# A fused attention, gated layer and soft mixture: a new order of the first loads and reductions, and a later place for the turn of P

## The chip, the cores and the metric

The kernel runs on one core of a Trainium2 chip. The metric is the device time of one execution in microseconds (us); the time of a kernel is the median of its runs. The core has a matrix engine (TensorE, PE in the profile, with its weight loads as PEld), VectorE (DVE), ScalarE (ACT), GpSimd (POOL) and a queue that issues most of the DMAs (SyncE, SP).

## The reference

Three layers follow each other. q, k and v have 8 batches, 12 heads, 448 tokens and 64 features per head, all float32.

```
q_n, k_n = rmsnorm(q, g_q), rmsnorm(k, g_k)
attn = softmax(q_n @ k_n.T / 8);  x = attn @ v             # per batch and head
x = (sigmoid(x @ w_gate) * (x @ w_val)) @ w_out            # 768 -> 1536 -> 768
logits = x @ phi                                           # 3584 x 32
slot_input = softmax(logits over tokens).T @ x
slot_out[e] = relu(slot_input[e] @ w1[e]) @ w2[e]          # 8 experts, 4 slots each
out = softmax(logits over slots) @ slot_out
```

w_gate, w_val and w_out come as float64: the kernel reads their bits as pairs of 32-bit words.

## The kernel before, in words

**Pairs.** Attention is worked in 48 pairs of heads (j, from 0), six to a batch. The first 12 pairs, two batches, are worked in float32: `prep_a` squares q and k (ScalarE for pair 0, GpSimd after that), `prep_b` sums the squares on VectorE (line 272, then a scale on line 275), `prep_c` raises the sums to the power -1/2 on GpSimd (line 305) and scales k, `prep_g` turns q and k with TensorE into tiles named qt, which ScalarE copies to qkt (lines 396 and 400). A pair then has seven score tiles, t0 to t6. Each runs through `score` (TensorE, lines 428 and 434, into a PSUM tile sc; four such buffers are shared with the other tiles of that pool), `soft_max` (VectorE, line 470, which also scales by a factor in ss), `soft_exp` (ScalarE, line 490, into a tile p or ps: two buffers of the first and three of the second, taken in turn), `soft_hi` (the turn of P: four transposes on TensorE, line 499, into a tile pq) and `soft_lo` (a copy out by ScalarE, line 532). When all seven are in, `weigh` sums the rows (rs, lines 576 and 582) and multiplies by v (av, line 590). The other 36 pairs use float16 halves and turn P by DMA.

**Weights.** The three weight matrices are brought from float64 bits to float32 by three VectorE instructions per block (lines 694, 697 and 700), their largest value is found by ScalarE (line 677) and spread over the partitions by a small TensorE product (`spread_max`, line 129, tile am) that VectorE reduces (line 133); then they are split into float16 halves (ScalarE lines 742 and 743, GpSimd line 744). w_gate and w_val come in twelve blocks f of 256 columns, from pair 1 on.

**The largest value of v.** For each batch the kernel needs the largest value of v. For batch 0 `v_first` loads v[0] whole (1344 KB), reduces it on VectorE (line 233), and spreads it with the same `spread_max` on TensorE.

**The gated layer** follows one batch behind: chains of 18 float16 products (line 805), in the order gate f=0, gate f=1, value f=0, value f=1, gate f=2 and so on, each evacuated by ScalarE (line 811, gate) or VectorE (line 816, value). The soft mixture works in between and at the end.

**What sets the order.** The program is an agenda: `at(g, fn)` puts a piece of work on a step g; a pair has 18 steps, or 28 and 16 in the second batch, and a step of the gated layer has six products. The gated layer begins at step M0 = 115. Up to step 259 a scheduler re-orders what the agenda issues, by a simulated time line, on each engine; from there the order is as issued. Each engine's queue is worked in order. Ahead of step 0 stands the beginning, in the order of the words in `ORD`: `sel` builds the identity matrix and the 16 blocks of a selection matrix that only the soft mixture uses, `g` loads the two gain vectors g_q and g_k (tile gl) and makes their product ggn and the scales from it, `qk0`, `qk1`, `v0`, `v1` load pairs 0 and 1, `a0` to `g0` prepare pair 0, `w` starts the first weight loads (tiles wr), `vf` is `v_first`, `phi` loads phi and makes four copies of it.

Of the kernel before, what the change touches and what calls it, by code (L numbers as in the profile page):

```python
# [2 lines left out]
KN=json.loads('{"NPRE": 6, "PS": 15, "GO": -4, "GS": 3, "WOF": 2, "WS": 4, "EW": 4, "RSL": 4, "XF": 12, "NX": 4, "VSPL": 5, "VO": 8, "SQA": 1, "MUV": 1, "LOV": 1, "XS": 144, "SF": 7, "AM": 100, "AMO": 100, "AMG": 100, "LEN": [28, 16, 16, 16, 16, 16], "PO": [0, 0, 5, 9, 10, 11, 15, 3], "SO": [0, 3, 6, 8, 11, 13, 15], "PJ": 8, "LOJ": 6, "LOI": [1, 4], "WN": 68, "GB": 2, "WB": 0, "QW": 0, "QO": 0, "QS": 0, "QL": 0, "PX": 2, "QX": 0, "SX": 1, "TX": 3, "LAG": 99, "TEND": 20, "XSL": [5, 4, 3, 2], "DUP": 2, "ACC": 1, "NWT": 0, "NWP": 1, "JQ": 12, "EQ": [0, 0], "NQV": 1, "ORD": "sel qk0 a0 g qk1 w b0 c0 d0 e0 f0 g0 a1 v0 vf v1 phi", "JP": 12, "EVP": [], "DGE": 0}')  # L3

# [6 lines left out]
F32 = mybir.dt.float32  # L11
# [3 lines left out]
AF = mybir.ActivationFunctionType  # L15
ALU = mybir.AluOpType
# [7 lines left out]
def kernel(  # L24
# [83 lines left out]
    def at(g, fn):  # L108
        agenda.setdefault(max(g, now[0]), []).append(fn)
# [107 lines left out]
    def vamax_spread(b):  # L217
        vam_t["ps", b] = spread_max(vam_t[b][:, 6:7], 1)
# [8 lines left out]
        sig_t[b] = sg  # L227

    def v_first():
        x = gt.rearrange("p f a s -> p (f a s)").bitcast(F32)[:, 0:6 * S]  # L230
        sp.dma_start(out=x, in_=v[0].rearrange("h s d -> (h s d)").rearrange("(p e) -> p e", p=128))
        t = smp.tile([128, 8], F32, tag="vam", name="vam")
        vec.tensor_reduce(out=t[:, 6:7], in_=x, axis=AX.X, op=ALU.max, apply_absolute_value=True)
        vec.tensor_scalar(out=t[:, 6:7], in0=t[:, 6:7], scalar1=1e-30, scalar2=None, op0=ALU.max)
        vam_t[0] = t
        vamax_spread(0)
        vamax_scale(0)

    def moe_scales(b):
        sg = sig_t[b]  # L240
# [1032 lines left out]
    if True:  # L1273
        vec.memset(nhalf1, -0.5)
        EW = KN.get("EW", 1)

        def gains():
            gl = p1.tile([128, 2, D], F32, tag="t3", name="gl", bufs=3)
            for i, g in enumerate((g_q, g_k)):
                sp.dma_start(out=gl[:, i, :], in_=g.unsqueeze(0).to_broadcast([128, D]))  # L1280
            gm = smp.tile([128, 4], F32, tag="wa", name="gm")
            vec.tensor_tensor(out=ggn, in0=gl[:, 0, :], in1=gl[:, 1, :], op=ALU.mult)
            vec.tensor_reduce(out=gm[:, 0:1], in_=ggn, axis=AX.X, op=ALU.max, apply_absolute_value=True)
            vec.tensor_scalar(out=gm[:, 0:1], in0=gm[:, 0:1], scalar1=1e-30, scalar2=None, op0=ALU.max)
            exponent(gm[:, 1:2], gm[:, 0:1])
            vec.reciprocal(out=gm[:, 2:3], in_=gm[:, 1:2])
            vec.tensor_scalar(out=ggn, in0=ggn, scalar1=gm[:, 2:3], scalar2=None, op0=ALU.mult)
            if JQ:
                for i in range(2):
                    vec.tensor_copy(out=gl[:, i, :], in_=ggn)  # L1290
                ps = ps_mm.tile([128, 128], F32, tag="mm", name="gt")
                pe.transpose(out=ps, in_=gl.rearrange("p i d -> p (i d)"), identity=ident)
                act.copy(gcol, ps[:, 0:1])
            for o, sign in ((nesc, -1), (esc, 1)):
# [148 lines left out]
```

## Time and profile before

| | |
|---|---|
| time, median of 3 runs | 1691.48 us (1683.35 to 1693.24) |
| the profiled execution's own time | 1691.47 us |
| its span, from the first to the last instruction | 1689.7 us |
| busy: PE, DVE, ACT, POOL | 1562.3, 1055.4, 936.6, 634.7 us |
| clock of TensorE granted, mean | 0.963 |
| first product of scores | 30.12 us after the span's start |
| first product of the gated layer | 168.2 us |

Outside the span lie 1.77 us of the profiled execution's time, and that time is the median. In a row of a timeline stand the start, the duration in us, the engine, the line of the kernel, the operation, what it writes and reads, and how many instructions were merged (a float32 product counts as two instructions); in brackets, how long the engine sat idle before it and what ended that wait. In a row by windows stand the stretch and its length, then the busy time and the number of instructions of PE, PEld, DVE, ACT and POOL, the granted TensorE clock, the busy share of the DMA engines and what they moved in GB/s.

### The profile page before, as it was taken

How to read it: one execution, taken by the hardware profiler on the slowest of the kernel's cores; microseconds unless marked ns; L12 is line 12 of the kernel's file. 1: busy time of each engine (PE TensorE's matmuls, PEld its weight loads, DVE VectorE, ACT ScalarE, POOL GpSimd, SP SyncE). 2: the span in 40 equal slices, each digit the busy share in tenths (PEclk: the TensorE clock that was granted, in tenths of full speed). 3: DMA queues.
4: the chain of work that ended last, by engine and by line, in shares of the span. 5: the costliest groups of instructions: out<-in, count | busy, mean ns of one | idle time of the engine just before them, and what ended most of it. 6: DMA issues, size and time to landing. Idle time of an engine off the chain costs nothing.

```text
span 1689.7 us, 26467 instructions
## 1 busy us (share of the span) xinstructions
PE 1562.3 (92%) x9065; PEld 777.8 (46%) x9065; DVE 1055.4 (62%) x2602; ACT 936.6 (55%) x1795; POOL 634.7 (38%) x725
## 2 busy tenths in 40 slices
PE   3887678999999999999999999999999999999985
PEld 1444334454454454545444545454545454555323
DVE  6677876545667777767776777677767663310214
ACT  3777668744766566656655665466656663211113
POOL 3445533336234535454545454535454530000000
PEclk9898789999999999999999999999999999999876
DMA  6344455325448755774688468756884566444899
GB/s 204 91 132 147 148 164 161 103 71 127 92 109 175 178 106 138 179 185 95 148 163 189 92 153 164 159 108 138 180 183 96 129 141 191 149 153 150 315 376 328
DMA packets 508021, 266.55 MB, mean 158 GB/s; under 512 B 403568, under 2 KB 476016, under 8 KB 507760
## 3 DMA queue, kind: packets, MB, share of 16 engines
q1 hardware_dynamic: 500976, 227.13, 53.6%
q10 hardware_dynamic: 6912, 37.75, 7.2%
q8 instruction: 71, 1.16, 0.3%
q14 instruction: 62, 0.51, 0.1%
HBM read 162.96 MB, written 15.73 MB: 106 GB/s over the span
## 4 chain that ended last, share of the span: by engine, by line
PE 48%; DVE 8%; ACT 8%; DMA 5%; issue 3%; SPq 2%; POOL 0%; ACTq 0%; POOLq 0%; DVEq 0%
PE mm L805 32%; DMA uni<-pst 4%; PE av L597 4%; PE sc L451 3%; DVE pst L548 2%; ACT pst L509 2%; PE so L961 2%; PE hp L1180 1%; PE tx L948 1%; ACT p L490 1%; DVE sc L470 1%; PE po L1232 1%; ACT sgf L811 1%; DVE ss L272 1%; ACT L490 1%
## 5 line engine op out<-in xcount | busy, mean ns | idle before, releaser
L805 PE MATMUL mm<-ck,wt 128*128 128x448 f16 x3456 | 706.1, 354 | 0.9 <-DVE ck L612 0.9
L805 PEld LDWEIGHTS <-wt 128*128 128x128 f16 x3456 | 330.7, 98 | 323.9 <-issue 40.2
L805 PE MATMUL mm<-gt,wo 128*128 128x448 f16 x1728 | 347.5, 353 | 2.5 <-DMA wo<-wos 2.4
L509 ACT ACTIVATE pst<-p,sm 128x448 f16<-128x448 f32 x252 | 168.2, 668 | 222.5 <-DVE sm L505 133.6
L548 DVE SCALAR_TENSOR_TENSOR pst<-p,sm,pst 128x448 f16<-128x448 f32 x252 | 204.6, 812 | 96.3 <-ACT pst L509 87.5
L511 POOL COPY pst<-pst 128x64 f16<-128x64 f16 x252 | 63.9, 254 | 516.7 <-ACT pst L509 516.7
L490 ACT ACTIVATE p<-sc,sm 128x448 f32<-128x448 f32 x286 | 179.6, 628 | 126.5 <-DVE sc L470 123.5
L805 PEld LDWEIGHTS <-wo 128*128 128x128 f16 x1728 | 166.4, 98 | 165.0 <-issue 12.6
L470 DVE TENSOR_SCALAR_CACHE_REDUCE sc<-sc,scal 128x448 f32<-128x448 f32 x252 | 171.5, 681 | 15.8 <-PE sc L451 9.3
L305 POOL TENSOR_TENSOR rr<-ss,nhalf 128x16 f32<-128x16 f32 x48 | 149.1, 3107 | 48.2 <-DVE ss L275 27.6
L451 PE MATMUL sc<-qkt 128*128 128x448 f16 x432 | 116.9, 353 | 0.2 <-DMA qkt<-uni 0.2
L502 DVE TENSOR_SCALAR sm<-sm 128x1 f32<-128x1 f32 x252 | 37.3, 148 | 100.8 <-ACT p L490 100.3
L597 PE MATMUL av<-uni 128*64 128x448 f16 (+1 forms) x792 | 89.8, 361 | 6.7 <-DMA uni<-pst 6.7
L821 DVE TENSOR_TENSOR gt<-sgf,gt 128x448 f16<-128x448 f32 x96 | 76.3, 795 | 11.2 <-ACT gt L820 11.1
L820 ACT CAST gt<-sgf 128x448 f16<-128x448 f32 x96 | 53.5, 557 | 52.4 <-DVE sgf L816 48.6
L816 DVE SCALAR_TENSOR_TENSOR sgf<-mm,fcomp,sgf 128x448 f32<-128x448 f32 x84 | 56.9, 678 | 38.6 <-PE mm L805 38.3
L811 ACT ACTIVATE sgf<-mm,kgate 128x448 f32<-128x448 f32 x96 | 58.3, 632 | 39.7 <-PE mm L805 39.1
L470 DVE TENSOR_SCALAR_CACHE_REDUCE sc<-sc,ss 128x448 f32<-128x448 f32 x84 | 56.2, 684 | 28.5 <-PE sc L434 24.6
L265 POOL TENSOR_TENSOR qn<-rq 128x512 f32<-128x512 f32 x47 | 59.4, 1264 | 33.6 <-DMA rq<-in_q_dram 28.8
L597 PEld LDWEIGHTS <-uni 128*64 128x64 f16 (+1 forms) x792 | 43.5, 110 | 56.3 <-issue 29.9
L811 ACT ACT_TABLE_LOAD x51 | 65.4, 1283 | 4.3 <-PE mm L805 3.4
L265 POOL TENSOR_TENSOR kn<-rk 128x512 f32<-128x512 f32 x47 | 54.7, 1164 | 30.2 <-PE qt L385 17.5
(230 smaller groups left out, 2092.6 us busy)
## 6 DMA issues: line engine op xcount, KB each, us to landing
wo<-wos ACTq DMA_DIRECT2D x48, 768.0 KB, 4.8
wt<-in_moe_w_dram SPq DMA_DIRECT2D x18, 1024.0 KB, 9.7
x<-in_moe_w_dram SPq DMA_DIRECT2D x12, 1024.0 KB, 10.7
vl<-in_v_dram SPq DMA_DIRECT2D x42, 224.0 KB, 2.7
rq<-in_q_dram SPq DMA_DIRECT2D x48, 192.0 KB, 2.7
rk<-in_k_dram SPq DMA_DIRECT2D x48, 192.0 KB, 2.8
wr<-in_moe_w_gate_dram SPq DMA_DIRECT2D x12, 768.0 KB, 4.4
wr<-in_moe_w_val_dram SPq DMA_DIRECT2D x12, 768.0 KB, 4.4
```

Source lines behind the costliest of these rows:

```text
L265: pool.tensor_tensor(out=x, in0=raw[j][i], in1=raw[j][i], op=ALU.mult)
L305: pool.tensor_tensor(out=rr, in0=ss, in1=nhalf, op=ALU.pow)
L451: pe.matmul(out=ps, lhsT=qk[:, 3 * h, 128 * t + 128:128 * t + 256], rhs=qk[:, 3 * h + 1 + n, TAIL:512], start=(n == 0), stop=(n == 1),)
L470: vec.tensor_scalar(out=ps, in0=ps, scalar1=ne, scalar2=3e38, op0=ALU.mult, op1=ALU.min, accum_out=sm[:, 1:2])
L490: act.activation(out=p, in_=ps, func=AF.Exp, scale=-1.0 if KN.get("ACC", 0) else esc, bias=sm[:, 1:2], accum_out=total)
L509: act.activation(out=st[:, 0:S], in_=p, func=AF.Copy, scale=sm[:, 3:4])
L511: pool.tensor_copy(out=st[:, S:S + TAIL], in_=st[:, 0:TAIL])
L548: ins = vec.scalar_tensor_tensor(out=st[:, S + TAIL:], in0=p, scalar=sm[:, 3:4], in1=st[:, 0:S], op0=ALU.mult, op1=ALU.subtract)
L597: pe.matmul(out=ps[64 * h:64 * h + 64, :], lhsT=vs[0:kk, hl, h, tv, :], rhs=pt[h][0:kk, tp, :], start=(n == 0), stop=(n == len(passes) - 1),)
L805: pe.matmul(out=ps, lhsT=l, rhs=r, start=(n == 0 and m == 0), stop=(n == last and m == len(terms) - 1))
L811: act.activation(out=sgm, in_=mm_t.pop(("g", f)), func=AF.Sigmoid, scale=kgate[:, b % 2, f:f + 1])
L821: later(2, lambda: vec.tensor_tensor(out=gt[:, f, 1, :], in0=gf, in1=gt[:, f, 0, :], op=ALU.subtract))
```

## The change

Two things change.

The beginning: the order of its words is new. The load of the gains is a word of its own, `gl`, stands first, and is issued by ScalarE instead of SP, followed by one small exponential on ScalarE (of a column that is overwritten later); their arithmetic `g` comes after `b0` and `w`. The identity comes after the loads of pair 0. The 16 blocks of the selection matrix and three of the four copies of phi are put on steps M0+20 and M0+30; phi's load goes straight into its first place. `v_first` only loads; its reduction goes on step 4, the spreading on 6, the scale on 8 (`VF`).

The turn of P: in the float32 pairs `soft_hi` comes six steps after a tile's scores instead of three, and `soft_lo` seven instead of four.

```diff
-"ORD": "sel qk0 a0 g qk1 w b0 c0 d0 e0 f0 g0 a1 v0 vf v1 phi"
+"ORD": "gl qk0 sel a0 qk1 w b0 g c0 d0 e0 f0 g0 a1 v0 vf v1 phi", "VF": 4
...
     def v_first():
-        x = gt.rearrange("p f a s -> p (f a s)").bitcast(F32)[:, 0:6 * S]
+        vam_t["x"] = x = gt.rearrange("p f a s -> p (f a s)").bitcast(F32)[:, 0:6 * S]
         sp.dma_start(out=x, in_=v[0].rearrange("h s d -> (h s d)").rearrange("(p e) -> p e", p=128))
+
+    def v_first_max():
         t = smp.tile([128, 8], F32, tag="vam", name="vam")
-        vec.tensor_reduce(out=t[:, 6:7], in_=x, axis=AX.X, op=ALU.max, apply_absolute_value=True)
+        vec.tensor_reduce(out=t[:, 6:7], in_=vam_t.pop("x"), axis=AX.X, op=ALU.max, apply_absolute_value=True)
...
-        vamax_spread(0)
-        vamax_scale(0)
...
-                (3, lambda i=i: soft_hi(j, i)),
-                (4, lambda i=i: soft_lo(j, i)),
+                (3 + 3 * (j < JP), lambda i=i: soft_hi(j, i)),
+                (4 + 3 * (j < JP), lambda i=i: soft_lo(j, i)),
...
+        def gains_load():
+            gl = first["gl"] = p1.tile([128, 2, D], F32, tag="t3", name="gl", bufs=3)
+            for i, g in enumerate((g_q, g_k)):
+                act.dma_start(out=gl[:, i, :], in_=g.unsqueeze(0).to_broadcast([128, D]))
+            act.activation(out=scal[:, 2:3], in_=nhalf1, func=AF.Exp)
+
         def gains():
-            gl = p1.tile([128, 2, D], F32, tag="t3", name="gl", bufs=3)
-            for i, g in enumerate((g_q, g_k)):
-                sp.dma_start(out=gl[:, i, :], in_=g.unsqueeze(0).to_broadcast([128, D]))
+            gl = first["gl"]
...
         def slots_to_columns():
-            pl = p1.tile([128, KD, NS], F32, tag="t3", name="pl", bufs=3)
-            sp.dma_start(out=pl, in_=phi.rearrange("(c p) s -> p c s", p=128))
-            for m in range(4):
-                vec.tensor_copy(out=phr[:, :, m, :], in_=pl)
+            sp.dma_start(out=phr[:, :, 0, :], in_=phi.rearrange("(c p) s -> p c s", p=128))
+
+        def more_columns():
+            for m in range(1, 4):
+                vec.tensor_copy(out=phr[:, :, m, :], in_=phr[:, :, 0, :])
...
         def make_sel():
             make_identity(nc, ident)
+
+        def blocks_of_sel():
             for i in range(4):
...
+        at(KN["VF"], v_first_max)
+        at(KN["VF"] + 2, lambda: vamax_spread(0))
+        at(KN["VF"] + 4, lambda: vamax_scale(0))
+        at(M0 + 20, blocks_of_sel)
+        at(M0 + 30, more_columns)
```

What the scheduler makes of it is seen in the rows of each engine, in order; the numbers behind names tell buffers and versions apart. First VectorE at the beginning: ss_204 before and ss_189 after belong to pair 1, vam is the largest value of v, wr a block of weights, am its spread value, and the rows of line 470 are t0, t1, ... of pair 0. Before:

```order
L309 TENSOR_SCALAR ss_204<-rr_241,scal_78 128x8
L233 TENSOR_REDUCE vam_214<-gt_89 128x1
L1303 COPY gt_89<-pl_228 128x6x32 x4
L234 TENSOR_SCALAR vam_214<-vam_214 128x1
L694 TENSOR_SCALAR gt_89<-wr_166 128x768
L133 TENSOR_REDUCE vam_214<-am_217 128x1
L697 SCALAR_TENSOR_TENSOR gt_89<-wr_166,gt_89 128x768
L121 TENSOR_SCALAR sg_220<-vam_214 128x1
L272 TENSOR_REDUCE ss_346<-qn_347 128x8
L700 SCALAR_TENSOR_TENSOR gt_89<-wr_166,gt_89 128x768
L225 RECIPROCAL sg_220<-sg_220 128x1
L470 TENSOR_SCALAR sc_234,sm_247<-sc_234,ss_132 128x448
```

And after, from the first row of line 470 on:

```order
L470 TENSOR_SCALAR sc_204,sm_217<-sc_204,ss_120 128x448
L697 SCALAR_TENSOR_TENSOR gt_89<-wr_135,gt_89 128x768
L470 TENSOR_SCALAR sc_206,sm_219<-sc_206,ss_120 128x448
L700 SCALAR_TENSOR_TENSOR gt_89<-wr_135,gt_89 128x768
L470 TENSOR_SCALAR sc_237,sm_253<-sc_237,ss_120 128x448
L235 TENSOR_REDUCE vam_234<-gt_89 128x1
L309 TENSOR_SCALAR ss_189<-rr_211,scal_78 128x8
L470 TENSOR_SCALAR sc_239,sm_255<-sc_239,ss_120 128x448
L1310 COPY gt_89<-gt_89 128x6x32 x3
L236 TENSOR_SCALAR vam_234<-vam_234 128x1
```

The reduction of v stood ahead of all rows of line 470; now t0 to t2 of pair 0 stand ahead of it and t3 behind it. The copies of phi stay there, and the 16 copies of sel stay VectorE's first work: the scheduler puts both earlier than their steps. On TensorE the spread of v's largest value (line 129) stood ahead of pair 0's first scores, and now stands behind its first four scores and three turns.

Second TensorE in the middle of pair 2, from its row sums on: pq are the turns, here of t2 and t3 (the first two pq below), sc_660 and sc_662 before, sc_628 and sc_630 after, are the scores of t4 and t5. Before:

```order
L582 MATMUL rs_611<-ident_75,su_385 64x128 x6
L576 MATMUL rs_611<-ident_75,su_385 64x64 x2
L590 MATMUL av_610<-wt_88,rv_224 64x448 x8
L499 MATMUL pq_643<-ident_75,p_637 128x128 x4
L499 MATMUL pq_648<-ident_75,ps_639 128x128 x4
L434 MATMUL sc_660<-qkt_486 128x448
L434 MATMUL sc_662<-qkt_486 128x448
L388 MATMUL qt_669<-ident_75,rq_412 64x128 x8
```

After:

```order
L582 MATMUL rs_579<-ident_75,su_361 64x128 x6
L576 MATMUL rs_579<-ident_75,su_361 64x64 x2
L590 MATMUL av_578<-wt_88,rv_199 64x448 x8
L434 MATMUL sc_628<-qkt_464 128x448
L434 MATMUL sc_630<-qkt_464 128x448
L499 MATMUL pq_632<-ident_75,p_617 128x128 x4
L499 MATMUL pq_637<-ident_75,ps_619 128x128 x4
L388 MATMUL qt_647<-ident_75,rq_382 64x128 x8
```

The two turns and the two scores change places; the turns of t0 and t1, ahead of the row sums, stay there in both.

Third VectorE some way into the gated layer: line 816 evacuates the fourth chain of line 805 (mm_1624 before, mm_1604 after), line 133 reduces the spread value of the weights f=6 (am_1523 before, am_1491 after). Before:

```order
L697 SCALAR_TENSOR_TENSOR gt_89<-wr_1534,gt_89 128x768
L272 TENSOR_REDUCE ss_1802<-kn_1805 128x8
L700 SCALAR_TENSOR_TENSOR gt_89<-wr_1534,gt_89 128x768
L133 TENSOR_REDUCE wa_1506<-am_1523 128x2
L816 SCALAR_TENSOR_TENSOR sgf_91<-mm_1624,sgf_91 128x448
```

After:

```order
L816 SCALAR_TENSOR_TENSOR sgf_91<-mm_1604,sgf_91 128x448
L275 TENSOR_SCALAR ss_1782<-ss_1782 128x16
L121 TENSOR_SCALAR fexp_81<-wa_1437 128x1
L770 RECIPROCAL wa_1437<-fexp_81 128x1
L771 TENSOR_SCALAR wa_1437<-wa_1437 128x1
L694 TENSOR_SCALAR gt_89<-wr_1502 128x768
L821 TENSOR_TENSOR gt_89<-sgf_91,gt_89 128x448
L697 SCALAR_TENSOR_TENSOR gt_89<-wr_1502,gt_89 128x768
L133 TENSOR_REDUCE wa_1476<-am_1491 128x2
```

The fourth chain's evacuation moved from behind that reduction to ahead of it. On TensorE itself 72 products of line 805 stood ahead of the spread of f=7's values, and now 90 do, a whole fifth chain more; those of f=6 now stand beside it.

More of the change, by code (lines that the diff above doesn't have):

```diff
@@ L2 @@
 import json
-KN=json.loads('{"NPRE": 6, "PS": 15, "GO": -4, "GS": 3, "WOF": 2, "WS": 4, "EW": 4, "RSL": 4, "XF": 12, "NX": 4, "VSPL": 5, "VO": 8, "SQA": 1, "MUV": 1, "LOV": 1, "XS": 144, "SF": 7, "AM": 100, "AMO": 100, "AMG": 100, "LEN": [28, 16, 16, 16, 16, 16], "PO": [0, 0, 5, 9, 10, 11, 15, 3], "SO": [0, 3, 6, 8, 11, 13, 15], "PJ": 8, "LOJ": 6, "LOI": [1, 4], "WN": 68, "GB": 2, "WB": 0, "QW": 0, "QO": 0, "QS": 0, "QL": 0, "PX": 2, "QX": 0, "SX": 1, "TX": 3, "LAG": 99, "TEND": 20, "XSL": [5, 4, 3, 2], "DUP": 2, "ACC": 1, "NWT": 0, "NWP": 1, "JQ": 12, "EQ": [0, 0], "NQV": 1, "ORD": "sel qk0 a0 g qk1 w b0 c0 d0 e0 f0 g0 a1 v0 vf v1 phi", "JP": 12, "EVP": [], "DGE": 0}')
+KN=json.loads('{"NPRE": 6, "PS": 15, "GO": -4, "GS": 3, "WOF": 2, "WS": 4, "EW": 4, "RSL": 4, "XF": 12, "NX": 4, "VSPL": 5, "VO": 8, "SQA": 1, "MUV": 1, "LOV": 1, "XS": 144, "SF": 7, "AM": 100, "AMO": 100, "AMG": 100, "LEN": [28, 16, 16, 16, 16, 16], "PO": [0, 0, 5, 9, 10, 11, 15, 3], "SO": [0, 3, 6, 8, 11, 13, 15], "PJ": 8, "LOJ": 6, "LOI": [1, 4], "WN": 68, "GB": 2, "WB": 0, "QW": 0, "QO": 0, "QS": 0, "QL": 0, "PX": 2, "QX": 0, "SX": 1, "TX": 3, "LAG": 99, "TEND": 20, "XSL": [5, 4, 3, 2], "DUP": 2, "ACC": 1, "NWT": 0, "NWP": 1, "JQ": 12, "EQ": [0, 0], "NQV": 1, "ORD": "gl qk0 sel a0 qk1 w b0 g c0 d0 e0 f0 g0 a1 v0 vf v1 phi", "JP": 12, "EVP": [], "DGE": 0, "VF": 4}')
 import concourse.bass as bass
@@ L1275 @@
         EW = KN.get("EW", 1)
+        first = {}
+        def gains_load():
[3 more added lines that the diff above has]
+            act.activation(out=scal[:, 2:3], in_=nhalf1, func=AF.Exp)
         def gains():
-            gl = p1.tile([128, 2, D], F32, tag="t3", name="gl", bufs=3)
-            for i, g in enumerate((g_q, g_k)):
-                sp.dma_start(out=gl[:, i, :], in_=g.unsqueeze(0).to_broadcast([128, D]))
+            gl = first["gl"]
             gm = smp.tile([128, 4], F32, tag="wa", name="gm")
@@ L1316 @@
         ops = dict(
-            sel=make_sel, qk0=lambda: load_qk(0), g=gains, qk1=lambda: load_qk(1), w=w_first,
+            sel=make_sel, gl=gains_load, qk0=lambda: load_qk(0), g=gains, qk1=lambda: load_qk(1), w=w_first,
             a0=lambda: prep_a(0), b0=lambda: prep_b(0), c0=lambda: prep_c(0), d0=lambda: prep_d(0),
```

## The prediction

> **What bounds the kernel now.** I first read busy time by stage, then TensorE's waits, then the timeline at the places found.
>
> ```profile
> 0.00:30.00 30.00, 4.04 (x23) 2.97 (x23) 17.49 (x49) 5.74 (x10) 12.92 (x16) 1.00 0.77 232
> 30.00:160.00 130.00, 108.34 (x593) 56.55 (x594) 97.82 (x229) 94.35 (x208) 59.28 (x46) 0.89 0.42 123
> 160.00:240.00 80.00, 56.13 (x271) 28.49 (x268) 63.66 (x121) 55.86 (x95) 33.90 (x23) 0.79 0.55 169
> 240.00:320.00 80.00, 69.37 (x398) 34.56 (x398) 50.72 (x117) 65.60 (x112) 32.64 (x24) 0.98 0.49 127
> 320.00:440.00 120.00, 117.56 (x700) 59.55 (x699) 60.55 (x149) 63.86 (x128) 49.91 (x52) 1.00 0.38 100
> ```
>
> From 320 us on TensorE is busy 117.56 of 120: it sets the end, and what is done sooner by then is kept. Ahead of 320 it worked 4.04 + 108.34 + 56.13 + 69.37 = 237.9 us and stood idle for 82. The question is how much of those 82 goes. What it waited for up to 440 us:
>
> ```profile
> PE am L129 <- ACT wt L677: 18.6, 3, 10.8
> PE pq L499 <- ACT p L490: 14.6, 11, 3.7
> PE pq L499 <- ACT ps L490: 14.0, 12, 2.7
> PE am L129 <- DVE vam L234: 12.5, 1, 12.5
> ```
>
> The last is the beginning, the two pq rows the turn of P (28.6), the first the weights.
>
> **The change, part by part.** *The beginning.* Ahead of the first scores, TensorE, VectorE, ScalarE and SP each show a piece of it:
>
> ```profile
> 29.40 0.79 PE L129 MATMUL am<-ident,vam 128*128 128x128 f32 x2 [12.45 <-DVE vam L234]
> ```
>
> ```profile
> 4.37 1.28 ACT L263 ACT_TABLE_LOAD   x1 [4.37 <-DMA rq<-in_q_dram]
> ...
> 16.98 0.59 ACT L400 COPY qkt<-qt 128x512 f32<-128x512 f32 x1 [1.25 <-PE qt L385]
> ```
>
> ```profile
> 4.59 0.59 SPq L1280 DMA_DIRECT2D gl<-in_g_q_dram  x1
> ...
> 13.53 0.59 SPq L231 DMA_DIRECT2D gt<-in_v_dram  x1
> ```
>
> The landing of gl, then of v[0], by the views of their two lines:
>
> ```profile
> DMA to landing us min/median/max: 3.7/4.6/5.4
> ```
>
> ```profile
> DMA to landing us min/median/max: 9.2/9.2/9.2
> ```
>
> ```profile
> 10.77 0.23 DVE L1282 TENSOR_TENSOR ggn<-gl 128x64 f32<-128x64 f32 x1 [3.16 <-DMA gl<-in_g_k_dram]
> 10.91 0.17 DVE L275 TENSOR_SCALAR ss<-ss 128x16 f32<-128x16 f32 x1
> ...
> 20.64 0.17 DVE L275 TENSOR_SCALAR ss<-ss 128x16 f32<-128x16 f32 x1
> ...
> 24.51 1.11 DVE L309 TENSOR_SCALAR ss<-rr,scal 128x8 f32<-128x8 f32 x1 [1.80 <-POOL rr L305]
> 25.53 2.94 DVE L233 TENSOR_REDUCE vam<-gt 128x1 f32<-128x2688 f32 x1
> ...
> 29.27 0.55 DVE L694 TENSOR_SCALAR gt<-wr 128x768 int32<-128x768 int32 x1
> ...
> 30.44 0.95 DVE L697 SCALAR_TENSOR_TENSOR gt<-wr,gt 128x768 int32<-128x768 int32 x1
> ...
> 37.58 0.69 DVE L470 TENSOR_SCALAR_CACHE_REDUCE sc<-sc,ss 128x448 f32<-128x448 f32 x1
> ...
> 40.41 0.69 DVE L470 TENSOR_SCALAR_CACHE_REDUCE sc<-sc,ss 128x448 f32<-128x448 f32 x1 [2.08 <-PE sc L434]
> ...
> 47.44 0.69 DVE L470 TENSOR_SCALAR_CACHE_REDUCE sc<-sc,ss 128x448 f32<-128x448 f32 x1 [0.24 <-PE sc L434]
> ...
> 50.60 0.69 DVE L272 TENSOR_REDUCE ss<-qn 128x8 f32<-128x512 f32 x1 [2.41 <-POOL qn L265]
> ```
>
> The qkt of pair 0 is ready at 16.98 + 0.59 = 17.57, and its scores start only behind the am of v: 12.5 us. That looks like 12.5 us to win; VectorE's queue allows less. Step by step:
>
> (a) L275 at 10.91 stands behind ggn, which waited 3.16 for gl. Issued first, gl lands no later than about 1.3 + 5.4 = 6.7 (SP takes 0.59 to issue one, and ScalarE issues two) instead of 10.7. The table load of 1.28 no longer waits for rq. How much earlier L275 comes lies between 1.2 (gl as slow as before, its arithmetic ahead) and 2.9 (nearly all of the 3.16); the pow on POOL, the scaling and the turn of k follow as before. A rule of the Trainium skill bears on this (DMA: Bandwidth & Descriptors, "Issuing engines are not separate DMA queues"): transfers issued by different engines share the same 16 DMA engines, and a second issuer saves only issue time. By it gl lands no faster than in its row, (a) is its low end, and the sum below would be 16 instead of 17; no run here shows it yet.
>
> (b) The work that VectorE has ahead of t0 after the change ends in before at L275 of pair 1, 20.64 + 0.17 = 20.8; so t0 at 17.9 to 19.6. t0, t1 and t2 with one L697 and one L700 between take 3 × 0.69 + 2 × 0.95 = 4.0 (L700 is of L697's size): the reduction of v begins at 21.9 to 23.6. Its data lands at 13.53 + 9.2 = 22.7, less 0.6 for each of the two issues of gl that leave SP: 21.6, so just in time. Before: 25.53.
>
> (c) From there to t4 it took 37.58 - 25.53 = 12.05. Out of this stretch go three L470 (2.1) and an L694, L697 and L700 (2.45); L309 (1.11) comes in: 8.6, so t4 at 30.5 to 32.2, which is 5.4 to 7.1 earlier.
>
> (d) From t4 to pair 1's t0 it took 47.44 - 37.58 = 9.9, with a wait of 2.08 for the scores of t5, which stood behind a turn. t4 and t5 are now issued together, so I take this away: pair 1's t0 is 7.5 to 9.2 earlier.
>
> (e) VectorE then waited 2.41 for the square of a later pair's q. In the changed order that row stands behind t3 of pair 1: some 2 more.
>
> That is 9.5 to 11.2; I take 10. The ends: 1.2, if only the SP issues count, and 12.45 + 3.16 = 15.6. The 16 copies of sel stay first on VectorE, idle then: nothing. The extra exponential brings the table load forward and hides under rq's transfer; uncovered it costs one table load, 1.28.
>
> *The turn of P.* Pair 2, where the order shows the swap, and two waits ahead of it:
>
> ```profile
> 68.03 0.66 PE L499 MATMUL pq<-ident,ps 128*128 128x128 f32 x4 [2.13 <-ACT ps L490]
> ...
> 72.73 1.11 PE L499 MATMUL pq<-ident,p 128*128 128x128 f32 x4 [1.57 <-ACT p L490]
> 73.78 1.55 PE L582 MATMUL rs<-ident,su 128*64 128x128 f32 x12
> ...
> 79.55 0.66 PE L499 MATMUL pq<-ident,p 128*128 128x128 f32 x4
> ...
> 80.57 1.02 PE L434 MATMUL sc<-qkt 64*128 64x448 f32 x4
> ```
>
> The two waits are those of the last tile of the pair before and of t1; in the changed order these turns stand ahead of the row sums as before, so the waits stay. What moves is t4 and t5 ahead of the turns of t2 and t3: 80.57 - 79.55 = 1.0 earlier, and VectorE, idle there, starts on them that much sooner. Four pairs (2 to 5) at 0.5 to 1.0, as some swap only one turn: 3. The swap puts the copies of t2 and t3 some 1.0 later, which only the pair's row sums, a whole stage on, wait for; so not below nothing. The ends are nothing and all waits of turns from 60 to 160 us:
>
> ```profile
> PE pq L499 <- ACT ps L490: 11.5, 9, 2.7
> PE pq L499 <- ACT p L490: 6.7, 6, 2.2
> ```
>
> that is 18.2; I stay near the low end because of the order. In pairs 6 to 11 products of the gated layer already lie between; of the 28.6 - 18.2 = 10.4 left I take 1, between 0 and 5.
>
> *The gated layer's start.*
>
> ```profile
> 176.68 4.33 PE L805 MATMUL mm<-ck,wt 128*128 128x448 f16 x22
> ...
> 196.17 0.80 PE L129 MATMUL am<-ident,wa 128*128 128x128 f32 x2 [10.84 <-ACT wt L677]
> ```
>
> TensorE stood 10.84 us behind the am of block f=7. Eighteen more products, at 4.33 / 22 = 0.197 each 3.5 us, now stand ahead of it and fill that wait. VectorE is queued behind the am of f=6, which now comes as much later; so 3, between 0 and 3.5.
>
> Sum: 10 + 3 + 1 + 3 = 17 of the profiled execution's 1691.47, which is the median of the runs too: **1674**. With each term at its nearer ends, 8 + 2 + 0 + 0.5 = 10.5 and 12 + 5 + 2 + 3.5 = 22.5, this case reaches from 1669 to 1681.
>
> **The rivals.** *The clock recovers.* The granted clock was 0.89 and 0.79 in two stages. A look at 70 to 75 us, and at row sums at full clock:
>
> ```profile
> 70.00:75.00 5.00, 3.38 (x20) 2.58 (x20) 4.21 (x17) 4.36 (x11) 3.53 (x2) 0.51 0.66 199
> ```
>
> ```profile
> 52.28 0.91 PE L582 MATMUL rs<-ident,su 128*64 128x128 f32 x12 [1.61 <-DVE wa L133]
> ```
>
> Row sums took 1.55 at the low clock and 0.91 at the full one. If fewer waits keep the clock up, up to 0.11 × 108.34 + 0.21 × 56.13 = 23.7 us of TensorE's work is in reach; half is 12: 1662. Against it: the waits ahead of the row sums stay. The Trainium skill (TensorE: Matmul & The Clock Gate, "HAM oscillation — how this bites in real kernels") has the clock fall after idle gaps of more than about 3.4 us; by it shortening gaps of 2 us gains nothing, and this rival would end at the 1674. The trace disagrees: it fell with gaps of 2.13 and 1.57, the longest of that stretch; so shorter waits than that rule asks for matter here, and the rival keeps a chance of 0.17.
>
> *The weights take it back.* VectorE is busy 63.66 of 80 from 160 to 240, mostly with weights, and TensorE waits for them (18.6). If that stage runs at VectorE's own pace, only VectorE's shift survives, some 6 of (c), and TensorE's gain turns into a longer wait for am: 1685. For it: those 18.6. Against: VectorE had 130 - 97.82 = 32 us idle in the stage before, so weights can move forward with the rest. 0.28.
>
> *The buffers of P run out: slower.* Five buffers hold P; a later turn holds up to four while the fifth is written. If ScalarE's exponential must wait for a turn, ScalarE, whose copies and qkt stand behind it, and VectorE after it, stop in every float32 pair. At 2.13 a pair, the longest wait above, 12 pairs cost 25.6: 1691.5 - 10 + 25.6 = 1707. It ends slower than before from 10 / 12 = 0.85 us a pair on. Against it stands nearly all that the exponential waited for from 40 to 280 us:
>
> ```profile
>   DVE sc L470: 18.9, 16
> ```
>
> No turn among them, and t0 and t1 are still turned ahead of the row sums. 0.09.
>
> **How the numbers follow.** Forecast 0.46, clock 0.17, weights 0.28, buffers 0.09. 1% of 1691.5 is 17 us, about what a measurement tells from none: the bound is 1674.6. Half of the forecast's case and most of the clock's lie below it, with the upper ends of the costs: faster 0.44. The other half and the weights are the same: 0.47. Slower 0.09. The range leaves out the slower case and the end of the clock's: 1658 to 1691; the forecast's own is 1669 to 1681.
>
> **What would show it.** (a), (b): the first row of line 470 near 18 to 20 instead of 32.90, the reduction of v at 22 to 24. (d), (e): pair 1's t0 near 39, and no wait for the square behind it. The turn: t4's line 470 within 1 us of the end of av, pq waits from 60 on little below 28. The gated layer: its first product near 155, the wait for am near 7 instead of 10.84. Wrong if the first product of the gated layer comes less than 8 earlier, if the clock from 30 to 160 rises over 0.95, or if line 490 waits for line 499.

## The result and the profile after

The changed kernel took 1663.45 us in the median of 4 runs (1662.35 to 1665.61) beside 1687.41 for the kernel before: 0.9849 of it, 95% interval 0.981 to 0.9889. Measured once more on another occasion it was 1666.89 beside 1690.21, 0.9856 (0.984 to 0.9872). So it is 1.5% faster, some 24 us. Forecast were 1674, and 1669 to 1681 for the forecast's own case; the time lies below that, inside the whole range of 1658 to 1691. The profiled execution of the changed kernel took 1665.61, with a span of 1663.8.

Busy time by stage of the changed kernel, in the columns used before (TensorE, its weight loads, VectorE, ScalarE, GpSimd, granted clock, DMA share, GB/s):

```profile
0.00:30.00 30.00, 13.73 (x53) 7.55 (x53) 21.76 (x63) 10.89 (x23) 12.24 (x16) 1.00 0.80 235
30.00:160.00 130.00, 113.08 (x646) 59.92 (x646) 101.53 (x238) 102.64 (x220) 68.87 (x52) 0.90 0.46 138
160.00:240.00 80.00, 56.92 (x285) 28.51 (x283) 60.36 (x116) 54.42 (x94) 33.92 (x21) 0.78 0.54 159
240.00:320.00 80.00, 73.11 (x423) 37.91 (x422) 53.27 (x126) 65.80 (x115) 28.18 (x23) 0.98 0.50 135
320.00:440.00 120.00, 117.81 (x705) 60.03 (x704) 67.03 (x153) 64.87 (x127) 50.31 (x54) 1.00 0.39 100
```

TensorE's idle time ahead of 320 us is 320 - (13.73 + 113.08 + 56.92 + 73.11) = 63.2, 19 less than the 82. Nearly 10 of those lie in the first 30 us (13.73 busy against 4.04). The clock has 0.90 and 0.78 where it had 0.89 and 0.79: it did not recover. What TensorE waits for up to 440 us:

```profile
PE am L129 <- ACT wt L677: 17.8, 3, 9.6
PE pq L499 <- ACT p L490: 14.1, 8, 3.7
PE gt L1298 <- DVE gl L1296: 8.3, 1, 8.3
PE pq L499 <- ACT ps L490: 4.8, 7, 1.5
```

The wait for v's maximum over the partitions (12.5) has shrunk to 2.1. The waits for turns of P fell from 28.6 to 18.9. The wait for the weights is where it was: 17.8 against 18.6.

The steps of the beginning, on VectorE and then on TensorE:

```profile
5.81 0.23 DVE L1288 TENSOR_TENSOR ggn<-gl 128x64 f32<-128x64 f32 x1 [2.71 <-DMA gl<-in_g_k_dram]
...
8.74 0.17 DVE L275 TENSOR_SCALAR ss<-ss 128x16 f32<-128x16 f32 x1
...
18.55 0.69 DVE L470 TENSOR_SCALAR_CACHE_REDUCE sc<-sc,ss 128x448 f32<-128x448 f32 x1
...
22.10 2.95 DVE L235 TENSOR_REDUCE vam<-gt 128x1 f32<-128x2688 f32 x1
24.97 0.22 DVE L309 TENSOR_SCALAR ss<-rr,scal 128x8 f32<-128x8 f32 x1
...
29.46 0.67 DVE L470 TENSOR_SCALAR_CACHE_REDUCE sc<-sc,ss 128x448 f32<-128x448 f32 x1
...
33.36 0.69 DVE L470 TENSOR_SCALAR_CACHE_REDUCE sc<-sc,ss 128x448 f32<-128x448 f32 x1 [0.23 <-PE sc L428]
...
35.80 0.69 DVE L470 TENSOR_SCALAR_CACHE_REDUCE sc<-sc,ss 128x448 f32<-128x448 f32 x1
...
40.68 0.69 DVE L272 TENSOR_REDUCE ss<-qn 128x8 f32<-128x512 f32 x1 [0.99 <-POOL qn L265]
```

```profile
15.45 3.36 PE L434 MATMUL sc<-qkt 64*128 64x448 f32 x8 [0.68 <-ACT qkt L400]
...
26.41 0.80 PE L129 MATMUL am<-ident,vam 128*128 128x128 f32 x2 [2.08 <-DVE vam L236]
27.14 1.87 PE L434 MATMUL sc<-qkt 64*128 64x448 f32 x4
...
76.62 1.11 PE L499 MATMUL pq<-ident,p 128*128 128x128 f32 x4 [1.69 <-ACT p L490]
...
79.38 1.55 PE L582 MATMUL rs<-ident,su 128*64 128x128 f32 x12
...
98.56 0.66 PE L499 MATMUL pq<-ident,p 128*128 128x128 f32 x4 [2.28 <-ACT p L490]
99.14 1.09 PE L582 MATMUL rs<-ident,su 128*64 128x128 f32 x12
...
147.23 2.44 PE L805 MATMUL mm<-ck,wt 128*128 128x448 f16 x12
...
183.77 0.79 PE L129 MATMUL am<-ident,wa 128*128 128x128 f32 x2 [9.56 <-ACT wt L677]
```

The first scores start at 15.45 instead of 30.12, t0 is at 18.55, t4 at 29.46, pair 1's t0 at 35.80, and the first product of the gated layer starts at 147.23, 21 us earlier than 168.2. But the am of f=7 comes at 183.77, only 12.4 earlier than 196.17: behind the first gated product 8.5 of the 21 were given back. Of these 8.5, 3.5 are the eighteen more gated products that now stand ahead of this am; 5 are lost. The two wt magnitudes that this am needs stand on ScalarE behind one of an output weight (hl), in the changed kernel and then in the kernel before:

```profile
181.95 0.84 ACT L677 ACTIVATE hl<-x 128x768 f16<-128x768 f32 x1 [5.67 <-DVE wa L734]
...
182.79 0.83 ACT L677 ACTIVATE wt<-gt 128x768 f16<-128x768 f32 x1
```

```profile
194.36 0.84 ACT L677 ACTIVATE hl<-x 128x768 f16<-128x768 f32 x1 [3.89 <-DVE wa L734]
```

### The profile page after: what moved, and what is told of

The parts are those of the page before. It is cut to its first block, busy times and chain, and to the rows that moved or that the text cites. A ratio compares the mean times of both kernels' runs of the same rounds, so it can differ in the third digit from the quotient of the medians.

```text
span 1663.8 us, 26455 instructions
## 1 busy us (share of the span) xinstructions
PE 1556.9 (94%) x9065; PEld 778.6 (47%) x9065; DVE 1055.3 (63%) x2601; ACT 936.3 (56%) x1796; POOL 636.3 (38%) x725
## 4 chain that ended last, share of the span: by engine, by line
PE 45%; DVE 9%; ACT 8%; DMA 5%; issue 3%; SPq 2%; POOL 0%; ACTq 0%; POOLq 0%; DVEq 0%
PE mm L805 31%; PE av L597 4%; DVE pst L548 2%; PE sc L451 2%; DMA uni<-pst 2%; ACT pst L509 2%; PE so L961 1%; PE hp L1180 1%; ACT p L490 1%; DVE sc L470 1%; DVE ss L272 1%; PE tx L948 1%; ACT sgf L811 1%; PE po L1232 1%; DVE gt L821 1%
## 5 line engine op out<-in xcount | busy, mean ns | idle before, releaser
L597 PE MATMUL av<-uni 128*64 128x448 f16 (+1 forms) x792 | 87.8, 357 | 6.0 <-DMA uni<-pst 6.0
L470 DVE TENSOR_SCALAR_CACHE_REDUCE sc<-sc,ss 128x448 f32<-128x448 f32 x84 | 56.4, 684 | 22.4 <-PE sc L434 17.5
```

What stands on the lines that cost most here:

```text
L470: vec.tensor_scalar(out=ps, in0=ps, scalar1=ne, scalar2=3e38, op0=ALU.mult, op1=ALU.min, accum_out=sm[:, 1:2])
L597: pe.matmul(out=ps[64 * h:64 * h + 64, :], lhsT=vs[0:kk, hl, h, tv, :], rhs=pt[h][0:kk, tp, :], start=(n == 0), stop=(n == len(passes) - 1),)
```

## The experiments

All kernels below were profiled too. This table, read from TensorE's rows, gives the start in us of five places: the first row sums (pair 0, line 582), those of pair 5, the am of f=7, the turn of u at line 923 (which the expectations call the last products of the first batch), and the end of the span. It serves all experiments.

| kernel | row sums, pair 0 | pair 5 | am, f=7 | line 923 | end |
|---|---|---|---|---|---|
| before | 52.28 | 158.92 | 196.17 | 436.77 | 1689.7 |
| before_again | 53.31 | 161.10 | 198.55 | 439.01 | 1690.6 |
| turn_only | 51.88 | 160.85 | 200.30 | 436.09 | 1689.7 |
| v_moved_only | 42.75 | 145.60 | 190.55 | 431.33 | 1680.5 |
| begin_only | 39.87 | 148.26 | 184.22 | 423.49 | 1679.4 |
| begin_only_again | 40.05 | 146.68 | 182.46 | 423.10 | 1670.5 |
| v_in_old_place | 43.15 | 146.78 | 185.76 | 419.27 | 1667.6 |
| turn_pairs_6_11 | 42.93 | 149.60 | 186.20 | 419.42 | 1666.3 |
| turn_pairs_0_5 | 39.15 | 135.15 | 176.36 | 417.65 | 1663.9 |
| changed | 38.95 | 139.12 | 183.77 | 417.72 | 1663.8 |
| changed_again | 39.91 | 136.56 | 180.67 | 413.18 | 1660.1 |

In v_in_old_place the same lines stand three further down. The two rows of one program show how far such places move by chance: by 0.2 to 4.5 us up to line 923, and by 0.9 to 8.9 at the end.

**Each part alone.** begin_only is the changed kernel with

```diff
-                (3 + 3 * (j < JP), lambda i=i: soft_hi(j, i)),
-                (4 + 3 * (j < JP), lambda i=i: soft_lo(j, i)),
+                (3, lambda i=i: soft_hi(j, i)),
+                (4, lambda i=i: soft_lo(j, i)),
```

> The new beginning, with the turn of P at its old distance (one step after the exponential). Theory (the two parts are separate, the beginning is the larger): the first row sums near 39 as in the changed kernel (52.28 before), the first product of the gated layer 13 to 16 earlier than 168.2, and at the end 12 to 16 us off the kernel before, some 1673. Rival 1 (the turn carries it): 4 to 8 us off, about 1681. Rival 2 (the weights take the beginning's gain back, since the wait for the am of f=7 grows by as much): the first gated product 13 to 16 earlier, but the end only 0 to 5 us off.

> The new beginning with the turn of P at its old distance, once more. If the turn is worth 6 to 10 us behind the new beginning, the ratio is 0.990 to 0.993 again, some 1674; if the first measurement of it was disturbed (10 us were lost between 423 and 764 in its profile) and the parts add, it comes to 0.987, some 1668. By the theory from the earlier runs, the am of block f=7 comes near 184 as in the changed kernel, and from there to the last products of the first batch it takes 239 to 241, as in every kernel that turns pairs 6 to 11 early, against 232.5 to 236 with the later turn.

Measured: 1674.42 beside 1690.18 (0.992, interval 0.989 to 0.995), and 1672.95 beside 1690.57 (0.9919, 0.9895 to 0.9943). By medians that is 15.8 and 17.6 us off, by the ratios 13.5 and 13.7: about the theory's 12 to 16, and neither rival holds. The second measurement agrees with the first. What TensorE waited for from 60 to 160 us in begin_only is still the turn, in places longer than before (5.4 where the longest was 2.7):

```profile
PE pq L499 <- ACT ps L490: 9.6, 5, 5.4
PE pq L499 <- ACT p L490: 2.6, 3, 1.4
```

turn_only is the kernel before with the same two lines changed the other way.

> The old beginning, with the turn of P three steps later. Theory: 3 to 6 us off the kernel before (4 pairs at 0.5 to 1.0 and the small waits for turns between 60 and 160 us), about 1683; the longest wait for a turn ahead of each pair's row sums (2.13 in pair 2) stays. Rival 1 (the turn carries it): 14 to 18 off, about 1671. Rival 2 (without the earlier start it is worth nothing, because TensorE waits for VectorE in these pairs): within 2 of the kernel before.

Measured: 1687.68 beside 1690.18, 0.9991 (0.9969 to 1.0013): 1.5 us by the ratio, nothing that can be told from no change. That is below the theory's 3 to 6, which the interval (up to 5) does not wholly exclude, and of the second rival's size. Its first gated product came at 156.36 instead of 168.17, but TensorE was not 12 us ahead: that product now stands ahead of the row sums of pair 5, and these came at 160.85, as late as in the kernel before (158.92 and 161.10). It was some 4 us ahead: it reached the am of f=7 at 200.30 - 15.54 = 184.8, where the kernel before reached it at 185.3, with eighteen more gated products (3.5 us) done. There it stood longer than before, 15.54 instead of 10.84. Rows of TensorE, ScalarE, VectorE and GpSimd:

```profile
156.36 4.56 PE L805 MATMUL mm<-ck,wt 128*128 128x448 f16 x15
160.85 0.88 PE L582 MATMUL rs<-ident,su 128*64 128x128 f32 x12
...
200.30 0.80 PE L129 MATMUL am<-ident,wa 128*128 128x128 f32 x2 [15.54 <-ACT wt L677]
```

```profile
198.48 0.84 ACT L677 ACTIVATE hl<-x 128x768 f16<-128x768 f32 x1 [10.47 <-POOL ss L311]
```

```profile
191.31 2.38 DVE L700 SCALAR_TENSOR_TENSOR gt<-wr,gt 128x768 int32<-128x768 int32 x1
...
197.43 0.96 DVE L700 SCALAR_TENSOR_TENSOR x<-wr,x 128x768 int32<-128x768 int32 x1
```

```profile
190.87 4.32 POOL L744 TENSOR_TENSOR wt<-gt,wt 128x768 f16<-128x768 f32 x2
```

ScalarE stood 10.47 us behind the magnitude of an output weight whose bits VectorE finished only at 197.43 + 0.96 = 198.4; the two it needed for f=7 stand behind it. (The view names GpSimd's ss as releaser, but hl reads x, and starts when x is done.) So the turn alone brings TensorE to a wait for VectorE and ScalarE sooner, and the am comes at 200.30, later than in either profile of before (196.17 and 198.55).

**The parts together, and which pairs.** changed_again is the changed kernel itself. turn_pairs_0_5 and turn_pairs_6_11 turn late in those pairs only:

```diff
-                (3 + 3 * (j < JP), lambda i=i: soft_hi(j, i)),
+                (3 + 3 * (j < 6), lambda i=i: soft_hi(j, i)),        # pairs 0 to 5
+                (3 + 3 * (6 <= j < JP), lambda i=i: soft_hi(j, i)),  # or pairs 6 to 11
```

(and `soft_lo` likewise).

> The changed kernel itself, beside the next three on one chip, so that they and the earlier experiments can be set against it. If the two parts only add (begin_only 0.992 and turn_only 0.9991 of the kernel before), it stands at 0.991, some 1675; if the turn is worth 10 us behind the new beginning and nothing behind the old one, it stands at 0.985 again, some 1664.

> The changed kernel with the later turn of P in pairs 0 to 5 only (those ahead of the gated layer); pairs 6 to 11 turn one step after the exponential as before. Theory (the turn's gain lies in pairs 2 to 5): within 2 us of the changed kernel; row sums of pair 5 near 139 as there (148.26 with the new beginning alone). Rival (it lies in pairs 6 to 11, between the products of the gated layer): 5 to 10 slower than the changed kernel.

> The changed kernel with the later turn of P in pairs 6 to 11 only. Theory: as the new beginning alone up to the gated layer (row sums of pair 5 near 148, first gated product near 155), and 0 to 2 faster than that kernel at the end, so 8 to 10 slower than the changed one. Rival (the gain lies in pairs 6 to 11): within 2 of the changed kernel.

Measured: 0.9856 (0.984 to 0.9872), 0.9862 (0.9848 to 0.9876; 1666.76) and 0.9873 (0.9852 to 0.9894; 1669.19). The first says that the parts don't simply add: 0.992 times 0.9991 is 0.991. The excess is 9 us by these ratios and 4 by the medians (23.3 against 16.7 + 2.5); at line 923 it is 4 in the changed kernel's profile and 8 in changed_again's. The intervals of the ratios only just bear it, and the medians alone would not. The second fits the theory. The third does not: with the turn late in pairs 6 to 11 only, row sums of pair 5 come at 149.60 as expected, but the end is only 2.3 slower than changed_again by medians (2.9 by the ratios), not 8 to 10. So the turn has a share in both halves, and they overlap.

Where the second half's share lies is seen in the stretch from the am of f=7 to line 923. Busy time there, in the kernel before, begin_only_again, turn_pairs_6_11 and changed_again:

```profile
196.17:436.77 240.60, 214.50 (x1201) 107.68 (x1201) 144.50 (x323) 159.22 (x287) 98.49 (x84) 0.94 0.45 123
```

```profile
182.46:423.10 240.64, 217.68 (x1201) 108.60 (x1201) 143.99 (x323) 159.35 (x287) 98.66 (x84) 0.93 0.45 123
```

```profile
186.20:419.42 233.22, 211.28 (x1184) 107.53 (x1184) 147.05 (x324) 158.97 (x286) 98.13 (x84) 0.94 0.46 127
```

```profile
180.67:413.18 232.51, 208.03 (x1184) 105.67 (x1184) 146.89 (x321) 158.48 (x286) 98.61 (x81) 0.96 0.46 126
```

The stretch takes 239.3 to 241.3 in all six kernels of the table that turn pairs 6 to 11 early, and 232.5 to 235.8 in all five that turn them late: between 3.5 and 8.8 less, 6.7 in the mean. TensorE has 17 instructions fewer in it, and up to the am 18 or 19 more: these are the eighteen products of the gated layer that now stand ahead of the am (3.5 us by their duration), where TensorE waits anyway. The other 3.2 are, in the mean of these kernels, 1.4 of shorter waiting and 1.8 of shorter busy time for the same instructions (in changed_again, at a granted clock of 0.96, TensorE even waits longer than in begin_only_again: 24.5 against 23.0). No run shows that the turn is what shortened it. Part of it is paid ahead of the stretch: turn_pairs_6_11 reaches the am at 186.20, begin_only at 184.22 and 182.46. Up to line 923 the turn is worth 423.3 - 417.65 = 5.6 in pairs 0 to 5, 3.9 in pairs 6 to 11, and 5.6 and 10.1 in the two profiles with both; without the new beginning 0.7 to 2.9.

**The reduction of v.** v_in_old_place is the changed kernel with `v_first_max`, `vamax_spread` and `vamax_scale` called at the end of `v_first` again; v_moved_only is the kernel before with only this move:

```diff
+        at(KN["VF"], v_first_max)
+        at(KN["VF"] + 2, lambda: vamax_spread(0))
+        at(KN["VF"] + 4, lambda: vamax_scale(0))
```

> The changed kernel with the reduction of v, its maximum over the partitions and its scale in their old place, ahead of the first scores. Theory (steps b to d: most of the beginning is the moved reduction): the first scores at 26 to 28 instead of 15.45, and at the end 8 to 12 us slower than the changed kernel, about 1673. Rival (the early gains, the table load and the columns of phi carry the beginning): at most 3 us slower, about 1666.

> The old beginning, with the reduction of v and what follows from it moved behind the first tiles' scores, as the changed kernel has it, and nothing else. Theory (steps c and d, and the changed kernel with v in its old place, which lost 4 us by the first row sums): the first scores near 17.6 instead of 30.12, the first row sums 4 to 7 earlier than 52.28, and 4 to 7 us at the end, some 1684. Rival (all of the beginning hangs on this move): the first row sums 12 to 13 earlier, and 13 at the end, some 1677.

Measured: v_in_old_place 1668.28 beside 1690.18, 0.9886 (0.9861 to 0.9911), so 1.4 us by the medians and 5 by the ratios slower than changed_again, not 8 to 12, and nearer to the rival's 3 at most; v_moved_only 1682.17 beside 1690.57, 0.9958 (0.9942 to 0.9974), 7 to 8.5 us faster than before, a little over the theory's 4 to 7 and far from the rival's 13. The first scores start at 25.61 (26 to 28 expected) and at 18.20 (17.6). TensorE of v_in_old_place, then of v_moved_only:

```profile
24.88 0.80 PE L129 MATMUL am<-ident,vam 128*128 128x128 f32 x2 [10.23 <-DVE vam L239]
25.61 2.61 PE L437 MATMUL sc<-qkt 64*128 64x448 f32 x6
```

```profile
18.20 3.35 PE L434 MATMUL sc<-qkt 64*128 64x448 f32 x8 [0.68 <-ACT qkt L400]
...
42.75 0.88 PE L582 MATMUL rs<-ident,su 128*64 128x128 f32 x12
...
190.55 0.79 PE L129 MATMUL am<-ident,wa 128*128 128x128 f32 x2 [15.18 <-ACT wt L677]
```

The move alone brings the first row sums 9.5 earlier, between the theory's 4 to 7 and the rival's 12 to 13, and those of pair 5 13.3; everything but the move (the turn too) brings the first row sums 9.1 earlier, all together 13.3. So each half of the new beginning can do two thirds of the work. And v_moved_only loses time at the same wait as turn_only: 13.3 us ahead at pair 5, TensorE then stands 15.18 for the weights, and 5.6 are left.

**The issuer of the gains.** gains_on_SP and gains_after_q differ from the changed kernel in one word each:

```diff
-                act.dma_start(out=gl[:, i, :], in_=g.unsqueeze(0).to_broadcast([128, D]))
+                sp.dma_start(out=gl[:, i, :], in_=g.unsqueeze(0).to_broadcast([128, D]))
```

```diff
-"ORD": "gl qk0 sel a0 qk1 w b0 g ...
+"ORD": "qk0 gl sel a0 qk1 w b0 g ...
```

> The changed kernel with the two loads of the gains issued by SP instead of ScalarE, in the same place, first of all. Theory (only issue time is saved by a second issuer): the gains land within 0.7 of 5.81, the first load of q is issued 1.2 later, and the first square of q starts 0 to 1.2 later than 6.21; at the end 0 to 1.5 us slower than the changed kernel, 1663.5 to 1665. Rival (the second issuer's own path is what makes the gains land early): the gains land at 8 or later, the first L275 2 or more later than 8.74, and 2 to 3 us slower at the end.

> The changed kernel with the loads of the gains issued behind those of the first q and k instead of ahead of them (still from ScalarE). Theory: ScalarE's queue is free, so they are issued at the same time and only the order in the program differs; the gains land within 0.7 of 5.81, and nothing changes by more than 1 us. Rival (their place at the head of the queue is what makes them land early, and it holds q back): q lands 1 to 1.8 earlier (its square begins near 4.4 to 5.2 instead of 6.21), the gains 2 to 4 later, the first L275 at 10.5 to 12.5 instead of 8.74, and 1 to 3 us slower at the end.

In gains_on_SP, VectorE's use of the gains, ScalarE's first square, and the landing of gl by the view of its tile:

```profile
5.44 0.23 DVE L1288 TENSOR_TENSOR ggn<-gl 128x64 f32<-128x64 f32 x1 [2.34 <-DMA gl<-in_g_k_dram]
```

```profile
6.47 0.63 ACT L263 ACTIVATE qn<-rq 128x512 f32<-128x512 f32 x1 [4.25 <-DMA rq<-in_q_dram]
```

```profile
DMA to landing us min/median/max: 3.5/3.8/4.1
```

The gains land as early as from ScalarE (5.44 against 5.81), and the first L275 comes at 9.22 against 8.74: the issuer saves half a microsecond. Its time, 1670.4 beside 1690.18 (0.9899, 0.9871 to 0.9927), is 3.5 above changed_again's by medians and 7 by the ratios, more than the theory's 1.5 and the rival's 3; but the rival's late landing does not appear, and at line 923 the kernel stands at 417.06, level with the changed one: what it loses comes after that, from a cause that stays open. gains_after_q, as expected, changes nothing that can be told from chance (first L275 at 8.80, line 923 at 419.93; 1667.58 beside 1690.57, 0.9872, 0.9852 to 0.9892).

**The wait for the weights.** output_weights_later is the changed kernel with `"WOF": 6` for `"WOF": 2`.

> The changed kernel with the preparation of the output weights begun 4 steps later. In the changed kernel TensorE waits 9.56 us for the am of block f=7; the two magnitudes on ScalarE that it needs stand there behind one of an output weight, whose data VectorE brings late. Theory (that order makes the wait, so the weights hold back what the earlier start won): the wait falls to 6 or less, the first product with the output weights comes 3 to 5 earlier than 327.3, and the end 2 to 5 earlier. Rival (VectorE's whole load of weights, busy 60.36 of 80 us, is what TensorE waits for): the wait falls here and comes back at a later am or at the first product with the output weights; end within 1.5 us of the changed kernel.

Waits for the am from 150 to 240 us, and busy time from 160 to 320, in this kernel:

```profile
PE am L129 <- ACT wt L677: 9.6, 4, 5.9
```

```profile
160.00:240.00 80.00, 64.16 (x317) 31.71 (x316) 56.00 (x116) 58.04 (x100) 33.36 (x21) 0.86 0.52 158
240.00:320.00 80.00, 69.04 (x397) 36.42 (x396) 48.91 (x116) 62.78 (x108) 26.76 (x21) 0.96 0.50 134
```

The waits fell from 17.8 to 9.6, and TensorE worked 64.16 of the 80 us instead of 56.92. But in the next 80 it worked 69.04 instead of 73.11, the first product with the output weights came at 326.59 (327.30 in the changed kernel, 322.72 in changed_again), and the end was 1667.42, 0.987 (0.9854 to 0.9885): no gain. The rival's size holds, but the wait came back in another place than it said: from 240 to 320 us TensorE waited 8.5 us for ScalarE's copies of turned tiles (line 532), against 3.8 in the changed kernel. So the order on ScalarE decides where TensorE waits; that VectorE's whole load of weights sets how long in all is not shown.

**The late part.**

> The kernel before against itself: a ratio of 1, and how wide its interval is. From the last products of the first batch (near 437 us) to the end it took 1253 in the kernel before and in turn_only, 1246 to 1251 in seven kernels with the new beginning and 1256 in begin_only. If the old beginning costs the late part 5 us, it takes 1252 to 1255 again here; if that difference is chance (the clock falling in one place or another), it can come out anywhere from 1246 to 1256.

Measured: 1690.87 beside 1690.57, ratio 1.0006 (0.9992 to 1.0019), and from line 923 to the end 1251.6. It was 1252.9 and 1253.6 in before and turn_only; v_moved_only has 1249.2, begin_only_again 1247.4, and the changed kernel 1246.1 and 1246.9 (begin_only's 1255.9 stands alone). So by these profiles 5 to 7 us of the gain lie past all the work that the change names. The profiles overstate it: they lie 28.2 us apart in the mean of two each, the medians 23 to 24, and with the 22.4 that line 923 shows little more than 1 of these would be left. Products av from line 923 on, before and changed_again:

```profile
L597 PE MATMUL av<-uni 128*64 128x448 f16 (+1 forms) x792 | 89.8, 361 | 6.7 <-DMA uni<-pst 6.7
```

```profile
L597 PE MATMUL av<-uni 128*64 128x448 f16 (+1 forms) x792 | 87.8, 357 | 6.9 <-DMA uni<-pst 6.9
```

Two of them are slower products av (89.8 us against 87.8 for the same 792). What starts it, and where the rest comes from, stays open.

## Why the prediction was right and wrong

- **(a)** L275 came 10.91 - 8.74 = 2.17 earlier, inside the 1.2 to 2.9, and the gains were used at 5.81, ahead of the 6.7. By the Trainium skill (DMA: Bandwidth & Descriptors, "Issuing engines are not separate DMA queues") a second issuer saves issue time only; gains_on_SP agrees (5.44 against 5.81). The sum of 16 that I drew from it was still wrong: the gains came early because they were issued early, which SP, with them first in its queue, does as well as ScalarE.
- **(b)** t0 at 18.55 (17.9 to 19.6) and the reduction of v at 22.10 (21.9 to 23.6) came as worked out.
- **(c), (d): mis-sized.** t4 came 8.1 earlier (5.4 to 7.1 said), pair 1's t0 11.6 (7.5 to 9.2). From the reduction to t4 VectorE took 7.4 where I had counted 8.6, and from t4 to pair 1's t0 6.3 instead of 9.9 - 2.08. Counting the instructions that leave VectorE's queue gave the first tile exactly and fell short by 1.2 and 1.5 us in the two steps after it. In (c) the largest part is L309, counted at the 1.11 of its row before; it took 0.22 at 24.97. In (d) I had taken away the wait for the scores of t5 alone; the wait for those of t6 behind it, 1.93 in the kernel before, shrank too, to the 0.23 at 33.36:

```profile
43.08 0.69 DVE L470 TENSOR_SCALAR_CACHE_REDUCE sc<-sc,ss 128x448 f32<-128x448 f32 x1 [1.93 <-PE sc L428]
```

- **(e) and the whole beginning.** The wait for the square of q shrank from 2.41 to 0.99. **The beginning, for which I took 10, measures 437.9 - 423.3 = 14.6 at line 923** (means of two profiles each) and 13.5 to 17.6 at the end. I had put most of it on the move of v; the runs show that either half of the new beginning brings about 9 of the 13.3 at the first row sums, the move or the rest.
- **The turn of P.** As said, the longest wait ahead of the row sums stays (2.28 at 98.56). But "pq waits little below 28" was wrong: they fell to 18.9 (17.3 in changed_again), and with the new beginning alone they are 23.4 and 24.9 in the two profiles of it, so the turn takes 5 to 7 off them. Of the 3 + 1 + 3 for pairs 2 to 5, later pairs and the gated layer, 7 in all, line 923 shows 423.3 - 415.4 = 7.9. That size is right, and the eighteen products (3.5) came as said. What I had not said is that it depends on the new beginning: alone the turn is worth 0.7 to 2.9 there.
- **The gated layer.** Its first product came at 147.2, earlier than the 155 said; the wait for am stayed at 9.56 instead of 7.
- **The rivals.** *The clock recovers* would have given 1662, near the time measured, by another way: the clock stayed at 0.90 and 0.78, so it did not decide there. In changed_again it had 0.93 and 0.81, which by the prediction's own reckoning is some 5 us, as much as that profile is ahead of the other at line 923 (4.5); so part of the 22.4 below can be the clock. The row sums at 79.38 still took 1.55 (granted clock 0.50 from 76 to 81), behind a wait of 1.69, the longest between 44 and 80 us. The rule of the Trainium skill (TensorE: Matmul & The Clock Gate, "HAM oscillation — how this bites in real kernels") that the clock falls after gaps of over some 3.4 us does not cover that row either. One reading of the prediction is wrong here: in the kernel before the clock stood at 1.00 from 69 to 70 us and at 0.53 from 70 to 71, so of its two waits the 2.13 lies ahead of the fall and the 1.57 behind it. *The weights take it back* is what happened in turn_only and v_moved_only, and it cost the changed kernel 5 of its 21 us; it fell as a forecast because with the whole change VectorE's unpacking moves forward too: the hl above starts at 181.95 instead of 194.36. *The buffers run out* did not happen: line 490 never waits for line 499.
- **The sum.** 17 were forecast for all that lies ahead of 440 us; the profiles show 19.1 in the first pair, and 22.4 in the mean of two of each. The rest up to the end, 23 to 24 by medians and 28 by the profiles, is the late part, of which no step spoke. The time fell inside the range because that was drawn wide for the clock, not because the sum was large enough.

## What to carry to other kernels

Ask of every gain on the busy engine which later wait it runs into, and whether the engine behind that wait is moved forward too: here TensorE's 21 us became 12 at the weights, and two edits that alone got TensorE some 4 and 13 us ahead kept 0.7 to 2.9 and 5.4 to 7.7 of it at the end of the first batch. Parts of a change that feed such a common wait need not add, so each has to be measured alone and together. An instruction that comes earlier need not mean that its engine is ahead: in turn_only it had only changed places with others. An order that lets one engine wait less in one place (the output weights) can simply move the wait on.

## What the hardware showed

- VectorE's unpacking (line 700, 128x768 int32, two inputs) takes 0.95 us in most places and up to 2.39 in others; at 191.31 in turn_only it runs beside GpSimd's subtraction of line 744. The Trainium skill (SBUF — State Buffer, "SBUF: two separate sides") has the two engines lock one pair of ports against each other for a whole instruction; the row fits that, though no run here took GpSimd's work away to prove it, and another of line 700 at 186.75 took 0.95 beside GpSimd's line 305. It can matter: from 187.62 on five VectorE operations of turn_only took 9.5 us, where the shortest rows of the same lines add up to 3.7, and the am behind them came 1.8 to 4.1 later than in the kernel before. That the one causes the other is not shown.
- TensorE's first scores ran at little over half speed for over 10 us: eight instructions in 3.36 us at 15.45 and four in 1.87 at 27.14 in the changed kernel, where four took 1.02 at 80.57 in the kernel before. The granted clock in the row of 0 to 30 us is 1.00 all the same, so that column does not show it.
- One program's places in the trace move by up to 4.5 us from run to run ahead of 440 us, and the times of one set of its runs span 3 to 18 us. Effects of a few us need many runs; the two pairs of profiles here lie 25.9 and 30.5 us apart in span, where the medians are 23 to 24 apart.
